# Clustered attention and two feed-forward layers on one core: value products held three units behind the scores, first-layer blocks in pairs, attention spread 18 units to a chunk

## The chip, the core and the metric

The kernel runs on one core of a Trainium2 chip. The core has five engines with a queue each: TensorE (PE, with its weight loads shown apart as PEld), VectorE (DVE), ScalarE (ACT), GpSimd (POOL) and SyncE (SP), which here only issues transfers. An engine takes its queue in order, and semaphores tell it when an operand is there. The metric is the time of one execution in microseconds; it is taken as the median of several timed runs.

## What is computed

Attention over 2 batches, 8 heads, 768 rows of 64 columns, in which a query sees only keys of its own cluster, and then two feed-forward layers over the 1536 rows of 512 columns that come out. Cut from the reference:

```python
q_assign = argmax(einsum(q_n, c_n)); k_assign = argmax(einsum(k_n, c_n))   # 16 clusters a head
scores = where(q_assign == k_assign, scale * q @ k.T, -1e9)
attn = softmax(scores)
x = attn @ v                                  # to [1536, 512]
h = x @ w_in;  x = (h / (1 + exp(-h))) @ w_out            # first layer, 512 -> 2048 -> 512
h = x @ w_in2; x = (max(h,0) + alpha*min(h,0)) @ w_out2   # second layer, the same sizes
```

The kernel keeps the accuracy of float32 by splitting each operand into two halves of 16 bits (high and low), and adds three products, high by high, high by low and low by high.

## The kernel before, in words

**Attention.** A unit is one head of one tile of 128 rows: 12 tiles by 8 heads, 96 units. `front(u)` makes the scores of a unit (four matmuls, L458 and L462, into one of two PSUM buffers `s`), takes the row maximum on DVE (L474) and two small columns (L477, L478), the exponential on ACT with its sum (L480), the high half on ACT (L487) and the low half on DVE (L489). `front_t(u)` sends both halves through a transposing transfer (L495) into one of three slots `pt`. `back(u)` makes the value products from the transposed halves (18 matmuls, L507) into the PSUM tile `x`. Two numbers couple them: `LAG = 2`, so that `back(u - 2)` is written behind `front(u)`, and `NPT = 3` slots. When the eight heads of a tile are done, `x_done` divides by the sums and splits the tile's result (L533, L536, L537) and transposes it (L538).

**First layer.** The 12 tiles are gathered in seven chunks (`CHUNKS`: two of one tile, five of two). For each chunk `layer1` makes 16 blocks of 128 hidden columns: 12 matmuls (L834), the nonlinearity from Tanh on ACT (L840), one DVE pass (L841), the high half on ACT (L844) and the low half on DVE (L845). Then come four groups of 48 matmuls of the second matrix (L865), each closed by a copy on ACT (L872). PSUM for these is a tile of two buffers (`w`), and a third (`m`) when attention is done.

**Weights.** The weights come as 64-bit numbers in pieces of 1 MB. Each is made into float32 by ACT, POOL (or ACT) and DVE (L572, L580 or L576, L583, L586), its squares are summed on ACT (L612), summed over the partitions by a matmul with the matrix `ones` (L211, `all_sum`), and split (L593 to L609). Pieces of the first matrix of a layer are split as they come; those of the second are split when all eight sums are there. The second layer's weights reuse the memory of attention: `w2_start` is called when all units are written, and its raw pieces lie where the keys lay, so that their loads (L561) wait for the last scores.

**Second layer.** `split_x2(j)` scales and splits a third of the first layer's result: four squares on ACT (L914) into a scratch `junk`, `all_sum`, four high halves on ACT (L923) and four low halves on DVE (L924). `layer2(j)` makes 16 blocks of 12 matmuls (L937, with L946, L947 on DVE, L950 on ACT, L951 on DVE behind them) and four groups of 48 matmuls (L968).

**Order.** The program is written chunk by chunk: 32 steps of a chunk's first layer, and between them units of attention so that `UNITS_BY_CHUNK` of them are written by the chunk's end. A scheduler then sets each engine's order by its own estimate of time, within the dependences; `issue_after` adds one that holds two instructions of an engine in order. All scratch memory is one arena of consecutive regions, `o_w` to `o_cw`; a place in it may be used by two things one after the other.

Of the kernel before, what the change touches and what calls it, by code (L numbers as in the profile page):

```python
# [23 lines left out]
UNITS_BY_CHUNK = (32, 53, 64, 69, 98, 98, 98)  # L24
# [22 lines left out]
def cluster_attention_silu_prelu(  # L47
# [61 lines left out]
    def region(nbytes):  # L109
        o = pos[0]  # L110
        pos[0] += nbytes
        return o
# [5 lines left out]
    o_tmp = region(3 * KB)  # L118
# [11 lines left out]
    o_xf = region(2 * KB)  # L130
# [118 lines left out]
    def prep_centroids2():  # L249
        craw = view(o_xf, F32, D)  # L250
        sq = view(o_xf + 256, F32, D)
        cc = view(o_xf + 512, F16, 3, 128)
# [192 lines left out]
    pt_of = {}  # L445
    x_ps = {}

    def front(u):
# [8 lines left out]
        for j in range(2):  # L457
# [4 lines left out]
            nc.tensor.matmul(  # L462
# [34 lines left out]
    def back(u):  # L497
# [7 lines left out]
        for t in range(T):  # L505
            for ph, vh in ((0, 0), (0, 1), (1, 0)):
                nc.tensor.matmul(  # L507
                    out=x_ps[0][:, h], lhsT=pt[:, ph * T + t], rhs=vt[:, h % 2, t, vh],
                    start=(i == 0), stop=(i == 3 * T - 1),
                )  # L510
                i += 1
# [8 lines left out]
    def x_done(n):  # L520
# [4 lines left out]
        xf = view(o_xf, F32, H, D)  # L525
# [12 lines left out]
        nc.sync.dma_start_transpose(  # L538
            out=view(o_xt + 4 * KB * (c % 3) + 2 * KB * i, F16, 2 * KD, 128),
            in_=xhl.rearrange("p a b -> p (a b)"),  # L540
# [173 lines left out]
    LAG = 2  # L714
# [89 lines left out]
    def layer1(c):  # L804
# [17 lines left out]
        for f in range(KF):  # L822
            j = f // 2
            wi = in_piece(o_w, j)
            if c == 0 and f % 2 == 0:
# [4 lines left out]
            hp = psum("l", n)  # L830
            i = 0
            for kd in range(KD):
                for a, bb in ((0, 0), (0, 1), (1, 0)):
                    nc.tensor.matmul(  # L834
                        out=hp, lhsT=wi[:, a, kd, f % 2 * 128:f % 2 * 128 + 128], rhs=mov(bb, kd),
                        start=(i == 0), stop=(i == 3 * KD - 1),
                    )
                    i += 1
            th = view(o_tmp + KB * ring("t1", 3), F32, n)
            nc.scalar.activation(out=th, in_=hp, func=ACTF.Tanh, scale=dh[:, f // 2:f // 2 + 1])  # L840
# [3 lines left out]
            nc.scalar.activation(out=g[:, f, 0], in_=th, func=ACTF.Copy, scale=2.0 ** -16)  # L844
            nc.vector.scalar_tensor_tensor(  # L845
                out=g[:, f, 1], in0=th, scalar=2.0 ** -16, in1=g[:, f, 0],
                op0=ALU.mult, op1=ALU.subtract,
# [218 lines left out]
```

## Time and profile before

| what | value |
|---|---|
| three timed runs | 874.54, 878.33 (median) and 878.88 us |
| the profiled execution | 873.64 us, its span 871.5 us |
| busy in the span | PE 81%, PEld 56%, DVE 70%, ACT 54%, POOL 18% |
| mean granted TensorE clock | 0.931 of full speed |

The page cuts the span into 40 slices. The first five or six hold the preparation of the first layer's weights, with DVE full and PE a quarter to half busy; from there to about 509 us attention and the first layer run side by side; to about 655 us the rest of the first layer runs beside the preparation of the second layer's weights; the remainder is the second layer, with PE full. Matmuls are pipelined, so that the mean duration of one is longer than the distance between two: the distance is read from a group of the chain of waits, its time over its count.

### The profile page before, as it was taken

The numbers are of one execution on the slowest core, as the hardware profiler recorded it, in microseconds if no ns is written. First come the engines' busy times: TensorE is split into PE (matmuls) and PEld (weight loads), VectorE is DVE, ScalarE is ACT, GpSimd is POOL, SyncE is SP. The second block draws the span as 40 slices with busy tenths as digits, with TensorE's granted clock in tenths as the row PEclk, the third lists the DMA queues.
The fourth block names the chain that finished last, engine by engine and source line by source line (L and its number), as shares of the span: only waits on it lengthen the run. The fifth ranks groups of instructions, "written<-read, shape, count | busy, mean of one in ns | idle before, by whom it ended". The sixth has DMA issues, their size and how long they took to land.

```text
span 871.5 us, 16209 instructions
## 1 busy us (share of the span) xinstructions
PE 704.7 (81%) x6484; PEld 487.1 (56%) x6484; DVE 607.4 (70%) x1302; ACT 468.5 (54%) x861; POOL 153.5 (18%) x117
## 2 busy tenths in 40 slices
PE   2435267777887997899898869789969999999998
PEld 1323146675766776788677758667424444444443
DVE  6999988888967777875986777786993058206700
ACT  7837576647857664755765577868541023002200
POOL 5734520340201220000000004341190000000000
PEclk9995567689999999999999999999999999999999
DMA  9999878659896786784778687353100000000000
GB/s 278 235 229 249 252 177 134 122 118 163 143 173 115 119 166 98 138 140 73 123 123 139 118 222 177 116 201 139 48 1 13 24 13 1 13 25 12 1 25 25
DMA packets 241595, 101.86 MB, mean 117 GB/s; under 512 B 217328, under 2 KB 227568, under 8 KB 241392
## 3 DMA queue, kind: packets, MB, share of 16 engines
q1 hardware_dynamic: 241520, 100.83, 54.0%
q8 instruction: 51, 0.84, 0.4%
q14 instruction: 24, 0.20, 0.1%
HBM read 44.08 MB, written 3.15 MB: 54 GB/s over the span
## 4 chain that ended last, share of the span: by engine, by line
PE 36%; DMA 12%; DVE 10%; ACT 4%; issue 2%; POOL 1%; SPq 0%; POOLq 0%; DVEq 0%; ACTq 0%
PE w L968 10%; DMA arena<-arena 8%; PE w L937 6%; PE m L968 5%; PE m L937 4%; PE w L865 3%; PE w L834 3%; DMA arena<-in_moe_w_out_dram 2%; PE x L507 2%; DMA arena<-in_moe_w_in_dram 2%; DVE arena L583 1%; DVE arena L586 1%; PE s L458 1%; PE s L462 1%; DVE arena L951 1%
## 5 line engine op out<-in xcount | busy, mean ns | idle before, releaser
L834 PEld LDWEIGHTS <-arena 128*128 128x128 f16 x1344 | 126.6, 107 | 35.1 <-issue 18.8
L834 PE MATMUL w<-arena 128*128 128x256 f16 (+1 forms) x1212 | 137.5, 273 | 10.6 <-DVE arena L841 8.5
L507 PE MATMUL x<-arena 128*128 128x64 f16 x1728 | 75.0, 202 | 79.9 <-DMA arena<-arena 78.9
L865 PEld LDWEIGHTS <-arena 128*128 128x128 f16 x1344 | 118.5, 100 | 20.7 <-POOL arena L605 2.9
L865 PE MATMUL w<-arena 128*128 128x256 f16 (+1 forms) x1200 | 123.9, 260 | 5.4 <-POOL arena L605 2.5
L507 PEld LDWEIGHTS <-arena 128*128 128x128 f16 x1728 | 66.2, 104 | 95.4 <-DMA arena<-arena 91.8
L489 DVE TENSOR_TENSOR arena<-arena 128x768 f16<-128x768 f32 x96 | 95.0, 991 | 32.3 <-ACT arena L487 32.0
L474 DVE TENSOR_REDUCE stat<-s 128x1 f32<-128x768 f32 x96 | 91.1, 951 | 28.4 <-PE s L462 28.2
L480 ACT ACTIVATE arena<-s,stat 128x768 f32<-128x768 f32 x96 | 94.5, 985 | 26.3 <-DVE stat L478 25.5
L487 ACT ACTIVATE arena<-arena 128x768 f16<-128x768 f32 x96 | 80.5, 842 | 42.0 <-DMA arena<-arena 41.0
L937 PEld LDWEIGHTS <-arena 128*128 128x128 f16 x576 | 57.0, 99 | 80.0 <-issue 15.5
L968 PEld LDWEIGHTS <-arena 128*128 128x128 f16 x576 | 56.4, 98 | 68.0
L580 POOL TENSOR_SCALAR arena<-arena 128x1024 f32<-128x1024 f32 x28 | 43.2, 1541 | 287.2 <-DMA arena<-in_moe_w_in_dram 219.1
L937 PE MATMUL w<-arena 128*128 128x512 f16 x384 | 87.7, 383 | 5.3 <-DVE arena L947 5.3
L458 PE MATMUL s<-arena 80*128 80x384 f16 x192 | 69.8, 364 | 17.6 <-DMA arena<-arena 11.1
L968 PE MATMUL w<-arena 128*128 128x512 f16 x384 | 83.9, 379 | 0.0
L950 ACT ACTIVATE arena<-arena,stat 128x512 f16<-128x512 f32 x48 | 34.5, 720 | 88.2 <-DVE arena L947 86.2
L462 PE MATMUL s<-arena 128*128 128x384 f16 x192 | 69.8, 364 | 0.0
L840 ACT ACTIVATE arena<-w,stat 128x256 f32<-128x256 f32 (+1 forms) x101 | 43.5, 434 | 29.3 <-PE w L834 24.2
L583 DVE SCALAR_TENSOR_TENSOR arena<-arena 128x1024 int32<-128x1024 int32 x32 | 42.9, 1340 | 22.1 <-ACT arena L572 8.3
L946 DVE TENSOR_SCALAR arena<-w,stat 128x512 f32<-128x512 f32 x32 | 24.0, 749 | 46.9 <-PE w L937 46.5
L845 DVE SCALAR_TENSOR_TENSOR arena<-arena 128x256 f16<-128x256 f32 (+1 forms) x112 | 49.7, 451 | 6.0 <-ACT arena L844 5.9
(137 smaller groups left out, 1014.1 us busy)
## 6 DMA issues: line engine op xcount, KB each, us to landing
arena<-in_moe_w_in_dram SPq DMA_DIRECT2D x16, 1024.0 KB, 5.9
arena<-in_moe_w_out_dram SPq DMA_DIRECT2D x16, 1024.0 KB, 5.1
arena<-in_k_dram SPq DMA_DIRECT2D x8, 384.0 KB, 3.8
arena<-in_q_dram SPq DMA_DIRECT2D x6, 512.0 KB, 4.9
arena<-in_v_dram SPq DMA_DIRECT2D x8, 384.0 KB, 5.8
out_dram<-arena SPq DMA_DIRECT2D x12, 256.0 KB, 2.0
arena<-arena SPq DMA_TRANSPOSE x149, 3.9
arena<-in_moe_alpha_dram SPq DMA_DIRECT2D x1, 1024.0 KB, 4.7
```

The lines of the kernel that those rows point to most:

```text
L458: nc.tensor.matmul(out=sc[:, j, :hs], lhsT=qt2[0:D + C, h], rhs=kt2[0:D + C, h % 2, j * hs:(j + 1) * hs], start=True, stop=False,)
L462: nc.tensor.matmul(out=sc[:, j, :hs], lhsT=qt1[:, h], rhs=kt1[:, h % 2, j * hs:(j + 1) * hs], start=False, stop=True,)
L474: nc.vector.tensor_reduce(out=nm, in_=sc[:, :, :hs], axis=AX.XY, op=ALU.max, negate=True)
L480: nc.scalar.activation(out=view(o, F32, 2, hs), in_=sc[:, :, :hs], func=ACTF.Exp, scale=scl, bias=bias, accum_out=sums[n % 2][:, h:h + 1],)
L487: nc.scalar.activation(out=hl[:, 0], in_=p, func=ACTF.Copy)
L489: en.tensor_tensor(out=hl[:, 1], in0=p, in1=hl[:, 0], op=ALU.subtract)
L507: nc.tensor.matmul(out=x_ps[0][:, h], lhsT=pt[:, ph * T + t], rhs=vt[:, h % 2, t, vh], start=(i == 0), stop=(i == 3 * T - 1),)
L583: nc.vector.scalar_tensor_tensor(out=lo, in0=hi, scalar=3, in1=lo, op0=ALU.logical_shift_left, op1=ALU.bitwise_or)
L834: nc.tensor.matmul(out=hp, lhsT=wi[:, a, kd, f % 2 * 128:f % 2 * 128 + 128], rhs=mov(bb, kd), start=(i == 0), stop=(i == 3 * KD - 1),)
L865: nc.tensor.matmul(out=acc, lhsT=wo[:, a, f % 2, dt * 128:(dt + 1) * 128], rhs=g[:, f, bb], start=(i == 0), stop=(i == 3 * KF - 1),)
L937: nc.tensor.matmul(out=hp, lhsT=in_piece(o_a + 24 * KB, f // 2)[:, a, kd, f % 2 * 128:][:, :128], rhs=x[bb][:, kd], start=(i == 0), stop=( ...
L968: nc.tensor.matmul(out=acc, lhsT=g[:, f, a, t * 128:(t + 1) * 128], rhs=out_piece(o_w, f // 2)[:, bb, f % 2], start=(i == 0), stop=(i == 3 ...
```

## The change

Four edits. (1) `LAG` goes from 2 to 3; the number of slots stays 3; and the first value product of a unit is told to stand behind the last score product of the unit three ahead. (2) `layer1` works on pairs of blocks: 24 matmuls into one PSUM tile of 512 columns, and then one Tanh, one DVE pass, one high half and one low half over both blocks (256 columns wide for the chunks of one tile, 512 for the others). The Tanh scratch grows from three buffers of 1 KB to two of 2 KB. (3) `UNITS_BY_CHUNK` goes from (32, 53, 64, 69, 98, 98, 98) to (32, 45, 63, 81, 99, 99, 99): 13, 18, 18 and 18 units in the second to the fifth chunk, where it was 21, 11, 5 and 29. (4) `x_done` works in two halves of four heads, with a scratch `xf` of 1 KB in place of 2 KB. The regions behind `o_xf` move 1 KB down in the arena: `o_xhl` to 82 KB, `o_one` (the matrices `ones` and `ident`) to 84 KB behind `o_a`. The scratch `junk` of `split_x2` keeps its address, 84 KB behind `o_a`, where the second half of `xhl` lay and where `ones` lies now.

```diff
-UNITS_BY_CHUNK = (32, 53, 64, 69, 98, 98, 98)
+UNITS_BY_CHUNK = (32, 45, 63, 81, 99, 99, 99)
...
-    o_tmp = region(3 * KB)
+    o_tmp = region(4 * KB)
...
-    o_xf = region(2 * KB)
+    o_xf = region(KB)
...
-            nc.tensor.matmul(
+            s_last[u] = nc.tensor.matmul(
...
-                nc.tensor.matmul(
+                mm = nc.tensor.matmul(
                     out=x_ps[0][:, h], lhsT=pt[:, ph * T + t], rhs=vt[:, h % 2, t, vh],
                     start=(i == 0), stop=(i == 3 * T - 1),
                 )
+                if i == 0 and u + LAG in s_last:
+                    issue_after(mm, s_last[u + LAG])
...
-        nc.vector.tensor_tensor(out=xf, in0=x_ps[0], in1=bc(rs, D), op=ALU.mult)
-        xf = view(o_xf, F32, DM)
-        xhl = view(o_xhl, F16, 2, DM)
-        nc.vector.tensor_copy(out=xhl[:, 0], in_=xf)
-        nc.vector.tensor_tensor(out=xhl[:, 1], in0=xf, in1=xhl[:, 0], op=ALU.subtract)
+        xhl = view(o_xhl, F16, 2, 2, DM // 2)
+        for w in range(2):
+            xf = view(o_xf, F32, 4, D)
...
-    LAG = 2
+    LAG = 3
...
-            hp = psum("l", n)
-            i = 0
-            for kd in range(KD):
-                for a, bb in ((0, 0), (0, 1), (1, 0)):
-                    nc.tensor.matmul(
-                        out=hp, lhsT=wi[:, a, kd, f % 2 * 128:f % 2 * 128 + 128], rhs=mov(bb, kd),
...
-            th = view(o_tmp + KB * ring("t1", 3), F32, n)
-            nc.scalar.activation(out=th, in_=hp, func=ACTF.Tanh, scale=dh[:, f // 2:f // 2 + 1])
+            hp = psum("l", 2, n)
+            for r in range(2):
+                i = 0
+                for kd in range(KD):
+                    for a, bb in ((0, 0), (0, 1), (1, 0)):
+                        nc.tensor.matmul(
+                            out=hp[:, r], lhsT=wi[:, a, kd, r * 128:r * 128 + 128], rhs=mov(bb, kd),
...
+            th = view(o_tmp + 2 * KB * ring("t1", 2), F32, 2, n)
+            nc.scalar.activation(out=th, in_=hp, func=ACTF.Tanh, scale=dh[:, j:j + 1])
...
-            nc.scalar.activation(out=g[:, f, 0], in_=th, func=ACTF.Copy, scale=2.0 ** -16)
+            hi, lo = g[:, 2 * j:2 * j + 2, 0], g[:, 2 * j:2 * j + 2, 1]
+            nc.scalar.activation(out=hi, in_=th, func=ACTF.Copy, scale=2.0 ** -16)
```

The new text has other line numbers: L458 and L462 become L459 and L463, L507 becomes L508, L834 becomes L841, L865 becomes L874, L612 becomes L619, L914, L923 and L924 become L923, L932 and L933, L937 becomes L946. The next pieces show the engines' queues.

On PE, around the last score products of all (L458, L462), which free the keys' memory; first before, then changed:

```order
L834 MATMUL w<-arena 128x256
L458 LDWEIGHTS arena [waits PE_49]
L458 MATMUL s<-arena 128x384 [waits Activation_49]
L462 LDWEIGHTS arena
L462 MATMUL s<-arena 128x384
```

```order
L874 MATMUL m<-arena 128x256
L459 LDWEIGHTS arena [waits PE_49]
L459 MATMUL s<-arena 128x384 [waits Activation_49]
L463 LDWEIGHTS arena
L463 MATMUL s<-arena 128x384
```

Before, they stand among the blocks of the sixth chunk's first matrix (L834); now among the sums of its second matrix (L874). Counted over the whole queue, 2004 matmuls of the first layer stand ahead of the scores of unit 93 before, and 2143 now. Between a unit's last score product and its first value product stand, for units 17 to 93 and with each matmul counted at its distance from the next in the trace, 12.3 us of PE's work on average before, and 15.2 now.

On ACT, the squares of `split_x2(0)` (L914, now L923) beside the sums of squares of the second layer's weights (L612, now L619) and their splits; first before, then changed:

```order
L603 ACTIVATE arena<-arena,stat 128x1024 [waits DVE_49,Activation_49]
L872 ACTIVATE arena<-w,stat 128x256 [waits PE_49]
L572 ACTIVATE arena<-arena 128x1024 [waits DMAHW0_49]
L604 ACTIVATE arena<-arena 128x1024 [waits Activation_49]
L872 ACTIVATE arena<-w,stat 128x256 [waits PE_49]
L914 ACTIVATE arena,stat<-arena 128x512 [waits DMAHW1_49,DVE_49]
L914 ACTIVATE arena,stat<-arena 128x512 [waits Activation_49] x2
L612 ACTIVATE arena,stat<-arena 128x1024 [waits DVE_49]
```

```order
L579 ACTIVATE arena<-arena 128x1024 [waits DMAHW5_49,Activation_49]
L619 ACTIVATE arena,stat<-arena 128x1024 [waits DVE_49]
L923 ACTIVATE arena,stat<-arena 128x512 [waits PE_49]
L923 ACTIVATE arena,stat<-arena 128x512 [waits Activation_49]
L610 ACTIVATE arena<-arena,stat 128x1024 [waits DVE_49]
L610 ACTIVATE arena<-arena,stat 128x1024
L923 ACTIVATE arena,stat<-arena 128x512 [waits Activation_49]
L611 ACTIVATE arena<-arena 128x1024 [waits Activation_49]
```

Before, the squares stand among the early pieces (L612 is that of the fourth of 16); now they stand behind the L619 of the last piece, and the first of them waits for PE, which reads `ones` for the pieces' sums. Twelve more ACT instructions of the splits and squares stand between the first square and the first high half (L932).

On PE, the sums over the partitions (L211) and the second layer's first blocks (L937, now L946); before, the last sum of the weights, then changed, the last three waits of them:

```order
L937 MATMUL w<-arena 128x512
L937 LDWEIGHTS arena
L937 MATMUL w<-arena 128x512
L211 MATMUL s<-stat,arena 128x1 [waits Activation_49]
L937 LDWEIGHTS arena [waits Pool_49]
L937 MATMUL m<-arena 128x512 [waits DVE_49]
```

```order
L211 MATMUL s<-stat,arena 128x1 [waits Activation_49]
L211 MATMUL s<-stat,arena 128x1 x2
L211 MATMUL s<-stat,arena 128x1 [waits Activation_49]
L211 MATMUL m<-stat,arena 128x1 [waits Activation_49]
L211 MATMUL m<-stat,arena 128x1 x3
L946 LDWEIGHTS arena [waits Pool_49]
L946 MATMUL m<-arena 128x512 [waits Activation_49]
```

Before, eight of the 16 blocks (96 matmuls) stand ahead of the last sum of the weights; now all 16 stand behind it, and behind the sum of `split_x2(0)` (the `m` row of L211).

## Rows read from the trace of the kernel before
**Rows 1.** Windows: microseconds of each engine busy in five stretches, PEclk granted clock.

```profile
75.00:100.00 25.00, 9.92 (x103) 6.43 (x104) 24.97 (x47) 14.49 (x22) 13.39 (x7) 0.50 0.92 248
125.00:509.00 384.00, 320.37 (x4090) 266.16 (x4089) 297.08 (x744) 247.53 (x501) 38.70 (x25) 0.94 0.75 130
509.00:623.00 114.00, 98.17 (x823) 76.91 (x821) 89.21 (x148) 82.45 (x151) 31.67 (x20) 0.97 0.53 164
623.00:659.50 36.50, 27.25 (x118) 12.10 (x116) 34.27 (x45) 17.21 (x23) 23.76 (x12) 0.91 0.00 1
659.50:871.50 212.00, 208.16 (x969) 94.69 (x967) 72.67 (x111) 35.12 (x50) 0.00 (x0) 1.00 0.04 15
```

**Rows 2.** Groups by line on PE, 125 to 200 and 200 to 509 us.

```profile
L507 PE MATMUL x<-arena 128*128 128x64 f16 x255 | 12.7, 214 | 12.4 <-DMA arena<-arena 12.3
...
L507 PE MATMUL x<-arena 128*128 128x64 f16 x1206 | 47.3, 194 | 33.9 <-DMA arena<-arena 33.1 <-DVE arena L533 0.7
```

**Rows 3.** The chain that ended last: start, duration, what, count.

```profile
376.69 3.84 DMA arena<-arena
380.57 0.70 PE x L507 x18
...
391.80 7.86 PE w L865 x72
...
703.68 5.18 PE w L937 x24
```

**Rows 4.** Groups by line and shape: busy, mean ns | idle before.

```profile
L845 DVE SCALAR_TENSOR_TENSOR arena<-arena 128x256 f16<-128x256 f32 x80 | 39.3, 495 | 5.7 <-ACT arena L844 5.7
L951 DVE SCALAR_TENSOR_TENSOR arena<-arena,stat 128x512 f16<-128x512 f32 x48 | 38.9, 812 | 4.8 <-ACT arena L950 4.6
L840 ACT ACTIVATE arena<-w,stat 128x256 f32<-128x256 f32 x69 | 32.2, 468 | 26.1 <-PE w L834 21.8 <-DVE arena L845 3.9
L841 DVE SCALAR_TENSOR_TENSOR arena<-arena,w 128x256 f32<-128x256 f32 x69 | 28.5, 414 | 5.0 <-ACT arena L840 5.0
L946 DVE TENSOR_SCALAR arena<-w,stat 128x512 f32<-128x512 f32 x32 | 24.0, 749 | 46.9 <-PE w L937 46.5
L947 DVE SCALAR_TENSOR_TENSOR arena<-w,arena 128x512 f32<-128x512 f32 x32 | 22.0, 687 | 0.3
L537 DVE TENSOR_TENSOR arena<-arena 128x512 f16<-128x512 f32 x12 | 9.7, 806 | 0.1
L533 DVE TENSOR_TENSOR arena<-x,stat 128x512 f32<-128x512 f32 x12 | 8.2, 683 | 2.6 <-PE x L507 2.6
L974 ACT ACTIVATE arena<-w,stat 128x512 f32<-128x512 f32 x8 | 5.5, 687 | 69.5 <-PE w L968 69.5
```

**Rows 5.** Timeline of ACT from 505 us: start, duration, what [idle before].

```profile
536.38 0.63 ACT L914 ACTIVATE arena<-arena 128x512 bf16<-128x512 f32 x1 [0.58 <-DMA arena<-arena]
...
621.79 1.14 ACT L612 ACTIVATE arena<-arena 128x1024 f32<-128x1024 f32 x1 [3.22 <-DVE arena L586]
...
629.13 2.17 ACT L603 ACTIVATE arena<-arena,stat 128x1024 f32<-128x1024 f32 x2
...
638.09 1.06 ACT L608 ACTIVATE arena<-arena 128x1024 f16<-128x1024 f32 x1 [0.82 <-POOL arena L607]
```

**Rows 6.** Timelines of DVE, POOL and PE from 590 us.

```profile
597.26 2.73 DVE L924 SCALAR_TENSOR_TENSOR arena<-arena,stat 128x512 f16<-128x512 f32 x4
...
645.67 2.60 DVE L924 SCALAR_TENSOR_TENSOR arena<-arena,stat 128x512 f16<-128x512 f32 x1
...
645.16 7.62 POOL L609 TENSOR_TENSOR arena<-arena 128x1024 f16<-128x1024 f32 x3
...
602.67 5.34 PE L937 MATMUL w<-arena 128*128 128x512 f16 x24
...
648.93 4.12 PE L937 MATMUL w<-arena 128*128 128x512 f16 x12 [4.22 <-DVE arena L947]
```

More of the change, by code (lines that the diff above doesn't have):

```diff
@@ L251, in prep_centroids2 @@
         sq = view(o_xf + 256, F32, D)
-        cc = view(o_xf + 512, F16, 3, 128)
+        cc = view(o_xhl, F16, 3, 128)
         ss, y, r = scr(1), scr(1), scr(1)
@@ L445, in cluster_attention_silu_prelu @@
     pt_of = {}
+    s_last = {}
     x_ps = {}
@@ L524, in x_done @@
         assert c < 3 or c - 3 in g1_done
-        xf = view(o_xf, F32, H, D)
         rs = scr(H)
@@ L532, in x_done @@
         )
-        nc.vector.tensor_tensor(out=xf, in0=x_ps[0], in1=bc(rs, D), op=ALU.mult)
-        xf = view(o_xf, F32, DM)
-        xhl = view(o_xhl, F16, 2, DM)
-        nc.vector.tensor_copy(out=xhl[:, 0], in_=xf)
-        nc.vector.tensor_tensor(out=xhl[:, 1], in0=xf, in1=xhl[:, 0], op=ALU.subtract)
+        xhl = view(o_xhl, F16, 2, 2, DM // 2)
+        for w in range(2):
+            xf = view(o_xf, F32, 4, D)
+            nc.vector.tensor_tensor(
+                out=xf, in0=x_ps[0][:, 4 * w:4 * w + 4], in1=bc(rs[:, 4 * w:4 * w + 4], D),
+                op=ALU.mult,
+            )
+            xf = view(o_xf, F32, DM // 2)
+            nc.vector.tensor_copy(out=xhl[:, 0, w], in_=xf)
+            nc.vector.tensor_tensor(out=xhl[:, 1, w], in0=xf, in1=xhl[:, 0, w], op=ALU.subtract)
         nc.sync.dma_start_transpose(
             out=view(o_xt + 4 * KB * (c % 3) + 2 * KB * i, F16, 2 * KD, 128),
-            in_=xhl.rearrange("p a b -> p (a b)"),
+            in_=view(o_xhl, F16, 2 * DM),
         )
@@ L821, in layer1 @@
             nc.vector.tensor_scalar(dh, w1["in"].inv, x_inv[b], 0.5, op0=ALU.mult, op1=ALU.mult)
-        for f in range(KF):
-            j = f // 2
+        for j in range(NPC):
             wi = in_piece(o_w, j)
-            if c == 0 and f % 2 == 0:
+            if c == 0:
                 nc.vector.tensor_scalar(
@@ L829, in layer1 @@
                 )
-            hp = psum("l", n)
-            i = 0
-            for kd in range(KD):
-                for a, bb in ((0, 0), (0, 1), (1, 0)):
-                    nc.tensor.matmul(
-                        out=hp, lhsT=wi[:, a, kd, f % 2 * 128:f % 2 * 128 + 128], rhs=mov(bb, kd),
-                        start=(i == 0), stop=(i == 3 * KD - 1),
-                    )
-                    i += 1
-            th = view(o_tmp + KB * ring("t1", 3), F32, n)
-            nc.scalar.activation(out=th, in_=hp, func=ACTF.Tanh, scale=dh[:, f // 2:f // 2 + 1])
+            hp = psum("l", 2, n)
[5 more added lines that the diff above has]
+                            out=hp[:, r], lhsT=wi[:, a, kd, r * 128:r * 128 + 128], rhs=mov(bb, kd),
+                            start=(i == 0), stop=(i == 3 * KD - 1),
+                        )
+                        i += 1
+                if r == 0:
+                    yield
+            th = view(o_tmp + 2 * KB * ring("t1", 2), F32, 2, n)
+            nc.scalar.activation(out=th, in_=hp, func=ACTF.Tanh, scale=dh[:, j:j + 1])
             nc.vector.scalar_tensor_tensor(
@@ L843, in layer1 @@
             )
-            nc.scalar.activation(out=g[:, f, 0], in_=th, func=ACTF.Copy, scale=2.0 ** -16)
+            hi, lo = g[:, 2 * j:2 * j + 2, 0], g[:, 2 * j:2 * j + 2, 1]
+            nc.scalar.activation(out=hi, in_=th, func=ACTF.Copy, scale=2.0 ** -16)
             nc.vector.scalar_tensor_tensor(
-                out=g[:, f, 1], in0=th, scalar=2.0 ** -16, in1=g[:, f, 0],
-                op0=ALU.mult, op1=ALU.subtract,
+                out=lo, in0=th, scalar=2.0 ** -16, in1=hi, op0=ALU.mult, op1=ALU.subtract,
             )
```

## The prediction

> **What bounds the kernel now.** I read the stretches first, to see where PE, the engine with most work, is not full; then PE's waits there; then the chain of waits, the price of the elementwise forms, and the timelines around the hand-over to the second layer.
>
> Four stages stand behind the preparation of the first weights. Stage 1 (125 to 509 us) ends with the last score products; PE works 320.4 of its 384 us [rows 1]. Of the 63.6 us idle, 12.3 + 33.1 = 45.4 us stand before the value products and wait for a transposing transfer [rows 2]; the chain shows one such step, the transfer of 3.84 us and the 18 products behind it [rows 3]. DVE is busy 297 us of the 384 and ACT 248: neither is full. Stage 2 (509 to 623 us) begins when the keys' memory is free for the second layer's weights and ends with the last piece's sum of squares (start 621.79, [rows 5]). No engine is full: PE 98.2, DVE 89.2, ACT 82.5 of 114 us [rows 1]. The pieces go through a ring of load, three engines, sum and split, in queues that they share with the first layer. Stage 3 (36.5 us, to the first L968) splits the second matrix and makes the blocks that are left; DVE is busy 34.3. Stage 4 (212 us) has PE at 208.2: nothing in it moves.
>
> So three things can change the time: what stands ahead of the last scores, how long the weights take behind them, and what is left to do when the last piece is summed.
>
> **The change part by part.** The sum is made on the profiled execution: span 871.5, with 2.14 us around it 873.64. The median of the timed runs is 878.33, 0.54% above; I carry the result over by that ratio.
>
> *Stage 1, more work.* By the queue of the changed kernel 2143 - 2004 = 139 more matmuls of the first layer stand ahead of the scores that free the keys. At 7.86/72 = 0.109 us each [rows 3]: +15 us.
>
> *Stage 1, fewer waits.* Between a unit's scores and its value products PE has 12.3 us of work on average now. With the idle share of the stage that is 12.3 x 384/320.4 = 14.7 us of elapsed time, and this is what the road through maximum, exponential, two halves and transfer takes, since PE waits at its end. Three units behind, the work alone is 15.2 us. On average the wait is covered, but 41 of the 77 units still have less than 14.7 us of work in the gap, where it was 63, and what is missing in all falls from 211 to 69 us. Shortfalls of neighbours are waited out together, so I take the ratio alone: 45.4 x (1 - 69/211), -31 us. The ends are -45 (all) and -12 (a quarter; the slots take the rest, below). What is late next is the slot: there are three, so the transfer of a unit now waits for the products of the unit three before it, and these stand behind its own scores. The transfer is ready some 9 us after those scores, and the products take 0.70 us [rows 3], so this is normally covered too; if it is not, a late product delays its slot's transfer and the delay goes on. SP takes its queue in order, so transfers and loads behind it wait as well.
>
> *Pairs of blocks.* A pair costs DVE 2 x (414 + 495) = 1818 ns now and, by the forms of 512 columns that the second layer has, 687 + 812 = 1499 ns after [rows 4]; ACT's Tanh goes from 2 x 468 to about 687 [rows 4]. For 40 pairs of full width DVE saves 13 us. In stage 1 I cost this at nothing: DVE has 87 us free there, and PE waits for transfers. In stage 2 it counts. The page Perfetto Trace Analysis of the Trainium skill, in Optimizing Scalar/DVE Operations, says that where these engines are not saturated but hold up another, smaller instructions let the work end sooner; by that rule pairing is a step the wrong way. The bound from rows: the first block's eviction starts 12 x 0.109 = 1.3 us later, 40 times 52 us if PE stood still for it. I take nothing, since in that time PE fills the other bank: 24 x 0.109 = 2.6 us against 687 + 687 ns until the bank is read out [rows 4]. By the page's rule the sum below would end up to those 52 us higher, by the rows at 864.
>
> *The result of a tile in halves.* Two passes of 683 and 806 ns [rows 4] become twice 414 and 495 ns or so, and the copy between them doubles its fixed part: 0.3 to 0.7 us for each of 12 tiles, 4 to 8 us of DVE. In stage 1 the free DVE time hides it. The last tile's is in stage 2, where PE has time to spare.
>
> *Stage 2, shorter.* DVE's 89.2 us lose 23 blocks of the first layer at 0.909 us and gain 8 pairs at 1.499 (the sixth chunk's blocks now stand before the last scores): -8.9. They lose six blocks of the second layer at 749 + 687 + 812 ns [rows 4]: -13.5, and one set of L924 [rows 6]: -2.7. That leaves 64 us, which at today's load would take 114 x 64/89.2 = 82 us. But the weights' sums still stand in PE's queue among the seventh chunk's 384 matmuls, and the chunk can't begin before the last unit's result. I take 95, between 82 and 114 (no gain): -19 us.
>
> *Stage 3, longer.* The scratch of the squares now lies on `ones`. The sums of all 16 pieces read `ones`, and they are written ahead of `split_x2(0)`, so its squares, which today start at 536.38 [rows 5], wait for the last piece, and all 16 blocks behind them; today eight are made ahead of the last sum, from 602.67 on [rows 6]. From the last sum of squares: 2 to 3 us to the first split; then ACT has the eight split instructions that take from 629.13 to 639.15 today [rows 5], and five squares of 0.8 us among them, before the first high half: 16 us. Then four L924. Alone they took 2.73/4 = 0.68 us each; beside POOL's L609, 2.60 [rows 6]. POOL is at those splits just then: 10 us. The first block ends near 27 us and 14 more follow at 5.18/24 x 12 = 2.59 us [rows 3]: 63 us, 64 with a slow first block (a block took 4.12 us after a wait, [rows 6]). So 64 in place of 36.5: +27.5 us. Without collision and queue it is 6 + 16 x 2.59 = 47 (+11); with two more slow blocks 68 (+31).
>
> *Sum.* 509 + 15 - 31 = 493; + 95 = 588; + 64 = 652; + 212 = 864 us of span, 866.1 with what lies around it, 7.5 us less than now. Times 878.33/873.64: 871 us, -0.9%.
>
> **Rivals.**
>
> *B, the ring runs free.* All 45.4 us of waiting go and stage 2 takes 82: 509 + 15 - 45 + 82 + 64 + 212 = 837, carried over 844 us. For it: the average gap already covers the road, and no engine is full in either stage. Against it: DVE, busy 77% of stage 1, would have to do nearly the same work in 350 us, 82%, and its queue is in order.
>
> *C, the clock falls in stage 2 (slower).* PE's work there shrinks to 545 matmuls, 59 us, while the stage lasts 95: 63% busy, in bursts between sums that it waits for. At 75 to 100 us PE was busy 9.9 of 25 us and the granted clock was 0.50, its lower level of 1.2 GHz; in stage 2 today, at 98 of 114, it is 0.97 [rows 1]. At the lower level the 59 us become 119, PE paces the weights, and the span is 493 + 119 + 64 + 212 = 888: 895 us. It decides from a granted clock below 59/95 = 0.62 in that stage. For it: every wait for a sum is an idle gap. Against it: 63% is nearer to the busy stage. The page TensorE: Matmul & The Clock Gate of the Trainium skill, in HAM oscillation — how this bites in real kernels, tells of matmuls that fall back to the cold clock at each wait for a transfer; by that rule C is the case.
>
> *D, the wait only moves.* With three slots at a lag of three, the road is held by its slot: PE waits in front of the value products as before, and a quarter of the 45.4 us goes: 509 + 15 - 12 + 95 + 64 + 212 = 883, carried over 890 us. For it: the lag grew and the slots did not, and the two buffers of the halves before the transfer are as they were. Against it: the products are in the queue right behind the scores that they follow.
>
> **How the numbers follow.** Forecast 0.47, B 0.17, C 0.13, D 0.23. The forecast alone spans 860 to 882: its wait term moves by 8 us and stage 2 by 8. Runs of this kernel differ by 0.5% (874.54 to 878.88), so less than 0.5%, 4.4 us, counts as no change. Faster: 0.31 of the forecast, all of B, 0.02 of D: 0.50. Within: 0.12 of the forecast, 0.01 of C, 0.05 of D: 0.18. Slower: 0.04, 0.12 and 0.16: 0.32. The range runs from just above B's middle to between D and C: 846 to 893; half of B, half of C and a fifth of D stay out.
>
> **What would show it.** Stage 1 right: idle time before the value products between 125 us and the last scores falls from 45 us to about 15, and the last scores come near 493 us. If it stays above 30, D. Stage 2 right: 90 to 100 us from the last scores to the last sum of squares, with a granted clock above 0.62; below it, C. Stage 3 right: no second-layer block before the last piece's sum; the squares of `split_x2(0)` behind it; L924 at about 2.6 us; and some 64 us to the first L968. Stage 4 at 212 us. The forecast is wrong if blocks of the second layer run ahead of the last sum, or if waits behind paired blocks on PE come to more than a few us in stage 1.

## The result and the profile after

The changed kernel takes 886.54 us (median, 883.32 to 888.1), the kernel before 876.43 beside it (873.41 to 878.88): ratio 1.0115, interval 1.0085 to 1.0146. It is slower, where 0.9% faster was forecast. The forecast of 871 lies 15.5 us below the time; the range, 846 to 893, held it.

The profiled execution has a span of 881.5 us. Its four stages, as windows (busy time of PE, PE's weight loads, DVE, ACT and POOL, granted clock, share of the transfer engines, GB/s); the ends are the last scores, the last piece's sum of squares and the first L977:

```profile
125.00:500.00 375.00, 329.93 (x4251) 277.93 (x4251) 291.25 (x695) 237.15 (x425) 38.33 (x25) 0.93 0.76 133
500.00:610.30 110.30, 66.96 (x614) 57.44 (x612) 75.02 (x98) 63.85 (x88) 30.33 (x20) 0.81 0.51 166
610.30:667.00 56.70, 45.44 (x199) 21.49 (x200) 47.05 (x65) 30.38 (x55) 22.81 (x12) 0.83 0.00 1
667.00:881.50 214.50, 210.73 (x981) 95.90 (x979) 73.89 (x113) 35.53 (x51) 0.00 (x0) 1.00 0.04 15
```

Beside [rows 1]: the last scores come 9 us sooner (forecast 16), stage 2 is 4 us shorter (forecast 19), stage 3 is 20 us longer (forecast 27.5), stage 4 longer by 2.5. In stage 2 PE works 67 of 110 us, and ACT and DVE are less busy than before as well: a stage in which work was taken out and PE, ACT and DVE all wait more.

PE's groups from 125 to 500 us (line, operation, count, busy time, mean ns, idle time before and what ended it), beside [rows 2]:

```profile
L508 PE MATMUL x<-arena 128*128 128x64 f16 x1442 | 57.3, 197 | 23.1 <-DMA arena<-arena 21.8 <-DVE arena L538 1.1
...
L459 PE MATMUL s<-arena 80*128 80x384 f16 x162 | 55.2, 341 | 8.4 <-ACT arena L481 8.0 <-DMA arena<-arena 0.3
```

The waits for a transposing transfer fell from 45.4 to 21.8 us, not to the 15 of the forecast, and the waits of the scores for the exponential (L481) rose from 2.4 to 8.0. The two elementwise forms of a pair on DVE, by line and shape, beside [rows 4]:

```profile
L855 DVE SCALAR_TENSOR_TENSOR arena<-arena 128x512 f16<-128x512 f32 x40 | 27.6, 693 | 5.0 <-ACT arena L854 4.8
...
L850 DVE SCALAR_TENSOR_TENSOR arena<-arena,w 128x512 f32<-128x512 f32 x34 | 23.2, 681 | 3.2 <-ACT arena L849 3.0
```

A pair costs DVE 681 + 693 = 1374 ns where 1499 was taken from the second layer's forms, so the pairs are no dearer than priced.

The chain that ended last, from the last pieces' loads to the second block of the second layer (start, duration, what), beside [rows 3]:

```profile
565.15 5.13 DMA arena<-in_moe_w_out_dram
...
570.45 1.13 POOL arena L587
...
571.60 1.24 DVE arena L590
...
572.86 1.24 DVE arena L593
...
574.12 1.23 ACT arena L619 x2
...
575.42 4.75 DMA arena<-in_moe_w_out_dram
...
589.65 5.00 DMA arena<-in_moe_w_out_dram
...
600.41 4.88 DMA arena<-in_moe_w_out_dram
...
609.11 1.20 ACT arena L619 x2
...
610.36 0.60 PE s L211 x2
...
610.98 0.73 ACT arena L923 x2
...
622.05 0.62 ACT arena L932
...
622.70 9.97 DVE arena L933 x4
632.67 0.04 issue
632.71 0.59 PE m L946 x2
...
635.24 2.59 PE m L946 x12
```

Two things stand in it. Up to 610 it is a ring of latency: a load of 5 us, four or five elementwise steps of about 1.2 us one after another, and only then the next load, because each load waits for a raw buffer that the sum (L619) of an earlier piece gives back. (These are pieces of the second matrix; a piece of the first holds its buffer until its split.) No engine is the bound there. And behind the last sum come, for the first time, the squares of `split_x2(0)` (L923), the high halves (L932) 12 us behind it, then the four L933 at 2.49 us each (9.97/4, the 2.60 of [rows 6]), and at 632.71 the products that wait for the last low half: 22 us of hand-over. PE has almost nothing to do in the first 12 of them, and makes 25 products of the second layer in the other 10:

```profile
610.30:622.70 12.40, 2.46 (x10) 2.31 (x11) 6.70 (x12) 11.69 (x21) 10.87 (x8) 0.50 0.00 0
622.70:632.70 10.00, 8.69 (x25) 3.10 (x25) 9.96 (x4) 3.86 (x9) 10.00 (x5) 0.64 0.01 2
```

### The profile page after: what moved, and what is told of

It is laid out like the page before. It is cut to its first block, busy times and chain, and to the rows that moved or that the text cites. A ratio compares the mean times of both kernels' runs of the same rounds, so it can differ in the third digit from the quotient of the medians.

```text
span 881.5 us, 16035 instructions
## 1 busy us (share of the span) xinstructions
PE 700.5 (79%) x6484; PEld 485.6 (55%) x6484; DVE 602.0 (68%) x1226; ACT 452.1 (51%) x749; POOL 144.7 (16%) x117
## 4 chain that ended last, share of the span: by engine, by line
PE 48%; DMA 20%; DVE 16%; ACT 7%; issue 5%; POOL 1%; SPq 1%; DVEq 0%; POOLq 0%; ACTq 0%
DMA arena<-arena 12%; PE w L977 9%; PE w L946 9%; PE w L841 6%; DMA arena<-in_moe_w_out_dram 6%; PE w L874 6%; PE m L977 5%; PE m L946 4%; PE x L508 3%; DVE arena L590 2%; DVE arena L593 2%; DVE arena L490 2%; PE s L459 2%; PE s L463 2%; DVE arena L601 2%
## 5 line engine op out<-in xcount | busy, mean ns | idle before, releaser
L841 PEld LDWEIGHTS <-arena 128*128 128x128 f16 x1344 | 120.6, 102 | 31.1 <-issue 13.2
L874 PE MATMUL w<-arena 128*128 128x256 f16 (+1 forms) x1248 | 129.9, 261 | 5.8 <-POOL arena L612 3.5
L841 PE MATMUL w<-arena 128*128 128x256 f16 (+1 forms) x1200 | 127.2, 263 | 6.8 <-DMA arena<-arena 4.5
L874 PEld LDWEIGHTS <-arena 128*128 128x128 f16 x1344 | 119.4, 101 | 20.7 <-POOL arena L612 3.8
L508 PE MATMUL x<-arena 128*128 128x64 f16 x1728 | 72.7, 202 | 52.5 <-DMA arena<-arena 44.6
L481 ACT ACTIVATE arena<-s,stat 128x768 f32<-128x768 f32 x96 | 94.2, 983 | 38.7 <-DVE stat L479 32.1
L508 PEld LDWEIGHTS <-arena 128*128 128x128 f16 x1728 | 66.4, 104 | 65.9 <-DMA arena<-arena 52.6
L946 PEld LDWEIGHTS <-arena 128*128 128x128 f16 x576 | 57.3, 100 | 73.4 <-issue 8.0
L977 PEld LDWEIGHTS <-arena 128*128 128x128 f16 x576 | 56.3, 98 | 68.0
L459 PE MATMUL s<-arena 80*128 80x384 f16 x192 | 70.5, 367 | 25.7 <-ACT arena L481 17.3
L946 PE MATMUL w<-arena 128*128 128x512 f16 x384 | 88.4, 384 | 0.0
L587 POOL TENSOR_SCALAR arena<-arena 128x1024 f32<-128x1024 f32 x28 | 37.5, 1339 | 291.7 <-issue 189.8
L977 PE MATMUL w<-arena 128*128 128x512 f16 x384 | 84.0, 379 | 0.0
L463 PE MATMUL s<-arena 128*128 128x384 f16 x192 | 71.0, 370 | 0.0
L590 DVE SCALAR_TENSOR_TENSOR arena<-arena 128x1024 int32<-128x1024 int32 x32 | 45.0, 1405 | 29.7 <-POOL arena L587 20.9
L619 ACT ACTIVATE arena<-arena 128x1024 f32<-128x1024 f32 x32 | 36.5, 1141 | 40.6 <-DVE arena L593 40.6
L579 ACT ACTIVATE arena<-arena 128x1024 int32<-128x1024 uint32 x32 | 36.3, 1134 | 35.0 <-DMA arena<-in_moe_w_out_dram 25.5
```

What stands on the lines that cost most here:

```text
L459: nc.tensor.matmul(out=sc[:, j, :hs], lhsT=qt2[0:D + C, h], rhs=kt2[0:D + C, h % 2, j * hs:(j + 1) * hs], start=True, stop=False,)
L463: s_last[u] = nc.tensor.matmul(out=sc[:, j, :hs], lhsT=qt1[:, h], rhs=kt1[:, h % 2, j * hs:(j + 1) * hs], start=False, stop=True,)
L481: nc.scalar.activation(out=view(o, F32, 2, hs), in_=sc[:, :, :hs], func=ACTF.Exp, scale=scl, bias=bias, accum_out=sums[n % 2][:, h:h + 1],)
L508: mm = nc.tensor.matmul(out=x_ps[0][:, h], lhsT=pt[:, ph * T + t], rhs=vt[:, h % 2, t, vh], start=(i == 0), stop=(i == 3 * T - 1),)
L590: nc.vector.scalar_tensor_tensor(out=lo, in0=hi, scalar=3, in1=lo, op0=ALU.logical_shift_left, op1=ALU.bitwise_or)
L841: nc.tensor.matmul(out=hp[:, r], lhsT=wi[:, a, kd, r * 128:r * 128 + 128], rhs=mov(bb, kd), start=(i == 0), stop=(i == 3 * KD - 1),)
```

## The experiments

All intervals are of the ratio to the kernel before, which took 874.4 to 875.4 us (medians) beside these runs. The table gives, from each profiled run, where the last score product, the last product of the first layer's first matrix, the first block of the second layer and the first output product start, and where the last piece's sum of squares is read.

| kernel | time, us | ratio (interval) | last scores | first matrix ends | first block | last sum | first output | span |
|---|---|---|---|---|---|---|---|---|
| before | 876.43 | | 509 | 579 | 603 | 623 | 660 | 871.5 |
| changed | 886.54 | 1.0115 (1.0085–1.0146) | 500 | 553 | 623 | 610 | 667 | 881.5 |
| changed, scratch moved | 854.08 | 0.9755 (0.9720–0.9791) | 500 | 553 | 579 | 618 | 633 | 849.7 |
| before, scratch on ones | 891.57 | 1.0190 (1.0153–1.0227) | 511 | 583 | 633 | 615 | 678 | 889.9 |
| changed, more buffers | 868.78 | 0.9930 (0.9899–0.9960) | 503 | 562 | 611 | 598 | 655 | 869.4 |
| before, more buffers | 874.17 | 0.9999 (0.9969–1.0030) | 512 | 592 | 619 | 607 | 661 | 873.4 |
| scratch moved, more buffers | 856.97 | 0.9785 (0.9747–0.9823) | 499 | 558 | 585 | 596 | 635 | 849.9 |
| before, lag 3 alone | 875.83 | 1.0003 (0.9976–1.0030) | 513 | 577 | 601 | 625 | 664 | 876.3 |
| before, pairs alone | 867.92 | 0.9899 (0.9866–0.9933) | 513 | 571 | 597 | 636 | 652 | 865.3 |
| before, spread alone | 871.05 | 0.9960 (0.9936–0.9984) | 501 | 597 | 620 | 614 | 663 | 874.5 |
| pairs and spread, scratch moved | 865.21 | 0.9868 (0.9821–0.9915) | 507 | 563 | 589 | 626 | 647 | 862.6 |
| pairs and lag 3, scratch moved | 858.91 | 0.9813 (0.9771–0.9855) | 501 | 558 | 585 | 614 | 644 | 855.5 |
| later spread, scratch moved | 855.20 | 0.9795 (0.9761–0.9829) | 506 | 560 | 583 | 619 | 637 | 852.9 |
| the same, more buffers | 854.21 | 0.9762 (0.9728–0.9797) | 506 | 561 | 589 | 597 | 639 | 853.6 |

### The scratch, taken off the ones and put on them

```
-        junk = view(o_a + 84 * KB, BF16, N2)
+        junk = view(o_tmp, BF16, N2)
```

> The changed kernel with one line different: the scratch of the squares of split_x2 lies in the first layer's scratch (o_tmp), no longer on the ones. Theory: the 57 us between the last weight piece's sum of squares and the first output matmul fall back to about the 37 us of the kernel before, since split_x2(0) and some 8 second-layer blocks run ahead of that sum again: about 866 us. Rival: the pieces hold the engines until then and hardly a block gets ahead: over 880 us.

Measured 854.08, ratio 0.9755: the line is worth 32 us, more than the theory's 20. Timelines by line of this run (count, min/median/max ns, first and last start), from 540 us:

```profile
L923 ACT ACTIVATE arena<-arena x12: 605/631/639, 560.2 to 586.3; 128x512 bf16<-128x512 f32 x12
...
L946 PE MATMUL m<-arena x72: 376/379/379, 579.4 to 631.9; 128*128 128x512 f16 x72
...
L977 PE MATMUL w<-arena x144: 376/379/390, 633.1 to 678.9; 128*128 128x512 f16 x144
...
L619 ACT ACTIVATION_READ_ACCUMULATOR arena<-arena x12: 173/186/208, 542.1 to 618.1; 128x1 f32 x12
```

The second layer's blocks begin at 579.4, right where the first layer's work ends, and run beside the weights. The last sum now comes 8 us later than in the changed kernel, and the first output product 34 us sooner: the last sum is not what the end waits for, once the blocks don't wait for it. PE in 575 to 600 and 600 to 625 us, first this kernel, then the changed one:

```profile
575.00:600.00 25.00, 22.98 (x127) 12.22 (x126) 22.47 (x28) 19.54 (x32) 4.92 (x4) 1.00 0.54 188
600.00:625.00 25.00, 22.13 (x102) 10.26 (x100) 23.58 (x43) 14.62 (x21) 4.17 (x4) 0.93 0.11 43
```

```profile
575.00:600.00 25.00, 4.43 (x34) 3.73 (x31) 12.26 (x10) 13.91 (x20) 5.06 (x4) 0.64 0.45 168
600.00:625.00 25.00, 5.34 (x19) 4.06 (x20) 11.45 (x15) 16.64 (x29) 14.26 (x10) 0.50 0.13 43
```

PE works 45 of these 50 us against 10: the 35 us are about the price of the line.

The same line the other way round, in the kernel before (`junk = view(o_one, BF16, N2)`):

> The kernel before with one line different: the scratch of the squares of split_x2 lies on the ones, as it comes to lie in the changed kernel. Theory: the 36.5 us from the last sum of squares to the first output matmul grow by about 20, and nothing else moves: about 896 us. Rival: the pieces before the sum get the engines for themselves, the sum comes sooner by as much, and the time stays within 5 us of 876.

891.57, ratio 1.0190: +17 us, so the theory, a little less than its 20. Its rows:

```profile
L914 ACT ACTIVATE arena<-arena x12: 612/629/631, 616.1 to 670.4; 128x512 bf16<-128x512 f32 x12
...
L937 PE MATMUL w<-arena x132: 376/379/379, 632.6 to 675.1; 128*128 128x512 f16 x132
...
L968 PE MATMUL w<-arena x48: 379/379/379, 677.9 to 688.1; 128*128 128x512 f16 x48
```

The squares start at 616 instead of 536 [rows 5], a microsecond behind the last sum. The price is half of that in the changed kernel, and the table shows why: here the first block comes 30 us late (633 for 603), because PE has first-layer work until then anyway; in the changed kernel that work is done at 578, and the first block comes 43 us late (623 for 579). What the pairs, the lag and the spread had gained was lost in front of one scratch buffer.

By the code, the line is also a fault of content. The scratch covers the 1 KB from 84 KB on, `ones` and `ident` both, so the squares overwrite `ones`, and the sum over the partitions in `split_x2` reads it behind them (in the changed kernel L923 from 610.98, L211 from 618.65). The scale of the second layer's input then comes from a wrong sum; no row here shows which scale came out.

### The ring of loads

```
...
-        raws = [o_a, o_a + 8 * KB, o_a + 16 * KB]
+        raws = [o_a + KB * i for i in (0, 8, 16, 56)]
...
-        w2["out"] = out_tasks(w2_out, raws, o_ts, o_w, w2["in"], "s", SPLIT[3], EXP_ON[3])
+        w2["out"] = out_tasks(w2_out, lambda j: o_a + KB * (68, 76, 0, 8, 16, 0, 8, 16)[j], o_ts, o_w, w2["in"], "s", SPLIT[3], EXP_ON[3])
...
-            w2["in"].loads + w2["in"].tasks + w2["out"].loads + w2["out"].tasks
+            w2["in"].loads + w2["out"].loads[:2] + w2["in"].tasks + w2["out"].loads[2:] + w2["out"].tasks
```

> The changed kernel, its scratch still on the ones, with the additional raw buffers alone. With the scratch on the ones, split_x2(0) waits for the last weight piece's sum of squares, and in this kernel alone should the ring's latency then set the end: the last sum comes some 20 us sooner (590 instead of 610) and the time falls to about 867 us. Rival (it is the engines' work on the pieces that holds the sum, with or without the ring): the sum moves by under 5 us and the time stays above 880.

868.78, ratio 0.9930, 18 us less than the changed kernel. The rows:

```profile
L923 ACT ACTIVATE arena<-arena x12: 612/629/631, 598.8 to 644.7; 128x512 bf16<-128x512 f32 x12
...
L977 PE MATMUL w<-arena x104: 379/379/379, 654.8 to 690.0; 128*128 128x512 f16 x104
...
L619 ACT ACTIVATION_READ_ACCUMULATOR arena<-arena x11: 178/194/291, 543.2 to 597.9; 128x1 f32 x11
...
502.90:597.90 95.00, 68.51 (x616) 57.17 (x614) 74.64 (x98) 64.22 (x88) 33.05 (x20) 0.88 0.59 194
```

The last sum comes at 598, 95 us behind the last scores, and everything behind it moves with it (57 us to the first output product, as without the buffers). DVE does the same work in the shorter stage (the window in the last row: 74.64 us, 75.02 in the changed kernel). So in the changed kernel the wait for buffers set stage 2, and stage 2 set the end.

> The kernel before with the same additional raw buffers. If the ring of loads had set the 114 us of stage 2 there too, as the rival of the forecast has it, they fall by 15 to 25 and the time to about 855 us. If DVE's queue of first-layer work set them, as the forecast's step said, they stay within 5 us and so does the time: 871 to 881.

874.17, ratio 0.9999. Half of each: the last sum comes 16 us sooner, and nothing behind it does.

```profile
L937 PE MATMUL w<-arena x132: 376/379/380, 619.1 to 658.5; 128*128 128x512 f16 x132
...
L968 PE MATMUL w<-arena x85: 379/379/379, 661.3 to 689.8; 128*128 128x512 f16 x85
...
L612 ACT ACTIVATION_READ_ACCUMULATOR arena<-arena x13: 178/188/218, 542.7 to 607.0; 128x1 f32 x13
...
607.00:661.30 54.30, 54.30 (x313) 30.59 (x312) 44.27 (x67) 26.30 (x41) 21.97 (x12) 1.00 0.00 1
```

The ring did hold the sum in the kernel before as well, but the end did not follow the sum: the weights now go ahead of the first layer on ACT and DVE, whose first matrix ends 13 us later, PE is full from the sum to the first output product (last row: 54.30 of 54.30 us), and that product stays at 661. Neither reading that I had put down for it is right: both took the last sum for the event that the rest waits for.

> The changed kernel with the scratch in o_tmp as in the run above, and more raw buffers for the second layer's weights: four for w2_in, and for w2_out five loads ahead of the first conversion instead of three. Theory (the load ring sets stage 2: each load waits for the sum of squares of the piece three before it, some 6.9 us a piece where the engines need about 3.4): stage 2 falls from 110 us to some 85 and the time to about 842 us. Rival (the engines' order and work set stage 2): stage 2 stays within 5 us of 110 and the time within 5 us of the run with the scratch alone.

856.97, ratio 0.9785 beside 0.9755, intervals overlapping: the rival's number. Stage 2 by its definition does shrink, 118 to 97 us, and it is worth nothing, as in the kernel before. The theory fell: it carried the 20 us of the scratch and the ring's 25 as two gains, but they are one wait. Take away what waits for the sum (32 us), or bring the sum forward (18 us); behind the first, the second gains nothing.

### The parts

Lag 3 alone in the kernel before (`LAG = 3`, the `issue_after` of the diff, units to 99):

> The kernel before with the lag of three alone (with its order of issue). If the waits for transposed probabilities are what the third unit removes and nothing takes their place, stage 1 ends 20 to 31 us sooner: 845 to 856. If single blocks on ACT and DVE then hold the units instead: 866 or more.

875.83, ratio 1.0003: nothing, the second case. The groups on PE from 125 to 500 us, of this kernel and then of the kernel before:

```profile
L837 PE MATMUL w<-arena 128*128 128x256 f16 (+1 forms) x1020 | 109.0, 261 | 9.2 <-DVE arena L844 8.9
...
L508 PE MATMUL x<-arena 128*128 128x64 f16 x1422 | 58.8, 198 | 36.2 <-DMA arena<-arena 35.4 <-DVE arena L536 0.7
```

```profile
L834 PE MATMUL w<-arena 128*128 128x256 f16 (+1 forms) x982 | 109.8, 271 | 2.5 <-DVE arena L841 2.4
...
L507 PE MATMUL x<-arena 128*128 128x64 f16 x1422 | 58.4, 198 | 42.6 <-DMA arena<-arena 41.6 <-DVE arena L533 0.7
```

Of 41.6 us before the value products 6.2 go, and PE's wait for DVE before the first layer's blocks grows by 6.5 in their place (2.4 to 8.9). All of PE's idle time from 125 us to the last scores is 64 us in both kernels.

Pairs alone in the kernel before (the loop of the diff, the halves of `x_done` that make the room, scratch in `o_tmp`):

> The kernel before with the pairs of column blocks alone (with the scratch in o_tmp, the halves of x_done that make the room, lag 2 and the spread of before). Elementwise work of the first layer falls by 25 us on DVE and as much on ACT in all; if it held the first layer back after the last scores, the first layer's end comes some 15 us sooner: 855 to 865. If the pairs gain only beside other work: within 5 us of 876.

867.92, ratio 0.9899. The last scores come 4 us later, the first matrix ends 9 us sooner, 57 us behind the scores instead of 70: the first case at its weak end, since the median lies above its 865 and the interval, 864 to 869 us, reaches it. (The squares of `split_x2(0)` start at 580 here instead of 536, since the scratch lies with the first layer's; what that is worth by itself was not tried.) The waits before the value products hardly change:

```profile
L507 PE MATMUL x<-arena 128*128 128x64 f16 x1386 | 57.1, 199 | 40.5 <-DMA arena<-arena 38.7 <-DVE stat L478 1.8
```

Lag 3 on top of the pairs (the changed kernel, scratch moved, `UNITS_BY_CHUNK = (32, 53, 64, 69, 99, 99, 99)`):

> The changed kernel with the scratch in o_tmp and the spread of units of before (32, 53, 64, 69, 99, 99, 99): pairs and lag alone. If the even spread pays for itself in stage 1 (139 first-layer matmuls moved ahead of the last scores, for fewer bare attention units after), this takes longer than the 854 us of the run with the scratch alone, by 3 to 10. If the spread only moves matmuls ahead of the last scores, as the term of +15 us has it, with the same matmuls lacking afterwards, within 3 us of 854.

858.91, ratio 0.9813: another 9 us below the pairs alone. Now the waits fall and none takes their place in full:

```profile
L508 PE MATMUL x<-arena 128*128 128x64 f16 x1440 | 57.5, 197 | 21.3 <-DMA arena<-arena 20.6 <-DVE arena L538 0.5
L459 PE MATMUL s<-arena 80*128 80x384 f16 x161 | 54.9, 341 | 9.5 <-ACT arena L481 8.9 <-DMA arena<-arena 0.5
```

The last scores move from 513 to 501. So the lag pays beside the pairs and not without them; that the wait before L837 is the whole reason is argued from these rows, not tried by itself. The run is also 4.8 us slower than the one with the even spread (their intervals overlap by a little): the spread gains there, by the number the first case. The reason given in that case does not hold. The even spread moves no matmuls of the first layer ahead of the last scores: counted in the traces, 2164 stand ahead of the scores of unit 93 in this run and 2143 with the even spread, and the last scores come at the same time. Where the gain behind them comes from is not shown.

> The changed kernel with the scratch in o_tmp and the values held two units behind the scores instead of three: pairs and spread alone. By the forecast's term (the third unit takes some 31 us of waits for transposed probabilities out of stage 1; 21 of them are gone in the trace of the changed kernel): 870 to 885 us. If the waits only went to other places: within 5 us of 854.

865.21, ratio 0.9868: between the two cases; its interval, 860 to 868 us, reaches neither. The third unit is worth 11 us here, not 31.

The even spread alone in the kernel before (`(32, 45, 63, 81, 98, 98, 98)`):

> The kernel before with the even spread alone (32, 45, 63, 81, 98, 98, 98). If the spread's 139 first-layer matmuls fill PE's waits before the last scores, it gains as it does with pairs and lag 3 (5 us): about 871. If at lag 2 with single blocks they only push the last scores back, 876 or more, with last scores at 515 or later.

871.05, ratio 0.9960: the first case by its number. The last scores come at 501, 8 us sooner and not later, but not because matmuls fill PE's waits. The even spread puts fewer of them ahead (1923 before the scores of unit 93, 2004 in the kernel before); up to the last scores PE is 9.5 us less busy than in [rows 1] and idle as long (65 us, 64 before):

```profile
125.00:501.00 376.00, 310.87 (x3996) 256.31 (x3995) 289.02 (x731) 242.44 (x489) 39.34 (x25) 0.93 0.77 133
```

The work is done later: the first matrix ends 17 us later. The profiled span, 874.5, does not show the gain of 0.4% that the timed runs have.

### A further version

Scratch moved, one chunk more spread among the units, two weight tasks a step (`(32, 42, 56, 70, 84, 99, 99)`, `W2_TASKS = 2`), and then with the additional buffers:

> The changed kernel with the scratch in o_tmp, the units spread over one chunk more (32, 42, 56, 70, 84, 99, 99) and two weight tasks a step. If the waits of PE before the last scores (some 120 us) can take another chunk's work of two layers, the last scores come little later than 500 and the first layer's end some 15 us sooner: about 840. If the spread works as the term of +15 us has it, the last scores move back by as much as the tail gets shorter, and the later start of the second layer's weights costs more: 860 to 880.

> The same with the additional raw buffers. If the weights' ring sets the end once there is less first-layer work behind the last scores, this is 10 to 20 us shorter than the run with that spread alone; if PE's work sets it, within 5 us.

855.20 and 854.21, ratios 0.9795 and 0.9762, with intervals that overlap that of the version with the scratch moved alone. The first lies in neither of its cases, the second in that of PE's work. The last scores move back by 6 us, and behind them some 3 are gained in the profiled runs (349 to 347 us to the end); the buffers again bring the sum forward (597) and no end. The best version is the changed one with its scratch moved, 2.45% below before; nothing tried on top of it was measurably better.

## Why the prediction was wrong, point by point

**Stage 2, shorter: the step that failed.** The forecast took the stage from 114 us to 95 for the work that leaves DVE. The work did leave (89.2 to 75.0 us busy), and the stage took 110.3. It was not set by that work: with more buffers it took 95.0 us (502.9 to 597.9) with the same work on DVE. What set it is the ring. The forecast had named it ("load, three engines, sum and split") and then priced it by the load of an engine instead of by the time for which a piece holds its buffer. That the run with more buffers meets the 95 and, with 868.78 us, comes near 871 is luck: 95 was taken between two bounds, for another reason.

How long a buffer is held is more than the links of the chain above. By those alone (10.3 us from one load to the next, three buffers) 16 pieces would take an estimated 55 us, half of the stage. The loads (L568) of the first matrix's eight pieces start over 61 us (492.3 to 553.6), and the splits give their buffers back; those of the second start over 45 us (555.5 to 600.4), and the steps between wait in queues that they share. How the 110 us divide among these waits was not worked out.

**The frame of the stages.** The sum took the last piece's sum of squares for the end of a stretch to which the next could be added, in the kernel before too. There it is no such boundary: 16 us sooner gave 0.01%. The profile's chain does run through it, but another is as long. PE is full from the end of the first matrix to that sum (22.94 of 23.40 us to the first block, 19.59 of 20.30 us from there); with the sum brought forward the first matrix ended 13 us later, and PE was full up to the first output product. Only the scratch on the ones makes everything behind wait for the sum. This error also hid the size of the scratch: its step says +27.5 us against a kernel before in which the blocks begin at 603, but in a kernel with pairs, lag and spread they would begin at 579, and the line costs 32.

**Stage 3, longer.** Right in mechanism, in every link that was named: squares behind the last sum, no block before it, four L933 at 2.49 us beside POOL. It took 57 us in place of 64, chiefly because the high halves began 12 us behind the sum and not 16. The page Perfetto Trace Analysis of the Trainium skill, in Optimizing Scalar/DVE Operations, says that GpSimd and DVE share a read port of the on-chip memory (SBUF); the rows agree with it, since the L933 of the run with the scratch moved took a median of 740 ns, and 2629 at most, the one that ran beside POOL's L612.

**Stage 1, fewer waits and more work.** Last scores at 500, forecast 493, because the wait term was too large. It was -31; the waits before the value products fell by 24, those of the scores for ACT rose, and PE's whole idle time from 125 us to the last scores fell by 18.6 us (63.6 to 45.1). The other term was +15 for 139 matmuls, and PE's busy time there grew by 9.6 us: -9 in place of -16. The matmuls came with the pairs and the lag, not with the spread. Counted in the traces, ahead of the scores of unit 93 stand 2004 before, 2107 with the pairs alone, 2164 with pairs and lag, and 2143 with the even spread on top. The pairs, costed at nothing in this stage, moved the last scores by +4.4 us, and the lag beside them by -12.8 (513.3 to 500.5).

**Pairs.** The 52 us of the bound did not come. In this stage PE waited 0.2 us for DVE before the paired blocks:

```profile
L841 PE MATMUL w<-arena 128*128 128x256 f16 (+1 forms) x1080 | 113.0, 262 | 4.8 <-DMA arena<-arena 4.5 <-DVE arena L850 0.2
```

The rule of the page Perfetto Trace Analysis of the Trainium skill, in Optimizing Scalar/DVE Operations, by which smaller instructions may let work end sooner that holds up another engine, had little to act on here: PE waited 2.4 us for DVE before the single blocks (L834, above), and the pairs alone made the kernel 1.0% faster.

**The sum.** 864 was forecast for the span and 881.5 measured: +7 in stage 1, +15.3 in stage 2, -7.3 in stage 3, +2.5 in stage 4. The sign was wrong by stage 2 alone: with its 95 us the sum would have been 866, below 871.5.

**The rivals.** B's free ring is not this kernel's: waits of 22 us stayed and stage 2 took 110, not 82. D's sign: 22 us is under its 30, so the wait was not merely moved to the slots, although a part of it did go to the scores (L459). The 890 us of D and the 895 of C lie nearer to the measured time than the forecast does, by causes that the runs do not bear out. C named the slower side: the granted clock in stage 2 was 0.81, above its 0.62, but 0.64 and 0.50 from 575 to 625 us, the lower of the two levels (1.2 of 2.4 GHz) toward the end. That agrees with the page TensorE: Matmul & The Clock Gate of the Trainium skill (HAM oscillation — how this bites in real kernels), by which matmuls fall back to the cold clock at each wait for a transfer; here PE waits for sums, and these for loads. The clock did not decide: PE worked 10 us in these 50 and waited for the ring, and with the scratch moved the clock in the same stretch is 1.00 and 0.93. The low clock was a sign of the wait, not its cause.

## What to carry over

When buffers are repacked, look up what every fixed offset (`o_a + 84 * KB`) now lies on: a scratch that lands on a constant makes its writer wait for all readers of that constant, and then overwrites it for the readers that follow; here it turned a gain of 2.45% into a loss of 1.15%. Before stretches are added up, ask what else is as long: if the event that closes one can come 16 us sooner without the time moving, it is no stage boundary. And a ring of few buffers is priced by how long a piece holds its buffer, from load to release and with the waits in queues, over the number of buffers, not by the busiest engine in it. Last, count what a change puts ahead of an event in each part by itself: the 139 matmuls were put down to the spread, which takes some away.

## What was not expected of the hardware

Between 75 and 100 us the granted clock differed between executions that did nearly the same. First the changed kernel, then the one with the scratch moved, whose work there is the same:

```profile
75.00:100.00 25.00, 8.88 (x88) 5.37 (x89) 25.00 (x49) 14.98 (x21) 12.38 (x8) 0.54 1.00 245
```

```profile
75.00:100.00 25.00, 9.64 (x89) 5.95 (x87) 25.00 (x46) 15.50 (x24) 13.25 (x8) 1.00 0.99 246
```

A PE that is 36% and 39% busy was given about half the clock in one run and all of it in the other. Of all fourteen profiled runs of this document, six have 0.50 to 0.57 in this stretch, with PE 36% to 40% busy, and eight have 1.00, with PE 36% to 42% busy. DVE was full in both of the runs shown, and the last scores came at 499.7 and 500.3. So the forecast's argument from 0.50 at 40% busy [rows 1] did not carry a rule, and the lower level cost nothing that can be seen where PE is not the bound.
